# Attention and a gated MLP in one kernel: the causal mask moved to GpSimd after the exponential, the first head's bias rows taken from the sums, and a load issued earlier

## The chip, the core and the metric

The kernel runs on one core of a Trainium2 chip. The core has a matrix engine (TensorE, in the profile PE, with its weight loads as PEld), a vector engine (VectorE, DVE), an activation engine (ScalarE, ACT), a programmable engine (GpSimd, POOL) and a queue engine (SyncE, SP). They run side by side, each through its own list of instructions in order, and wait for each other on semaphores. DMA transfers are issued from SP, ACT or POOL. The metric is the time of one execution on the device in microseconds.

## The reference, cut to what matters

The first half is attention over 8 batches of 8 heads, 576 positions and 64 features a head. To each score comes a bias that is made from running sums of a gate s, and the scores above the diagonal are shut out:

```
s_pos = np.maximum(s, 0.0)
cum = np.cumsum(s_pos, axis=-1)
bias = -(cum[:, :, :, None] - cum[:, :, None, :])
scores = np.where(causal, -1000000000.0, scores + np.minimum(bias, 0.0))
attn = np.exp(scores - max); attn = attn / (sum + 1e-09)
x = attn @ v
```

The second half is an MLP over the 4608 tokens so made (8 heads of 64 are 512 features): `h = x @ w_in` (2048 wide), `g = h * clip(h + 3, 0, 6) / 6`, `out = g @ w_out`.

## The kernel before, in words

**Pairs of heads.** The 64 heads are worked on two at a time. The main loop runs over 32 pairs p, numbered from 0; the ninth is p = 8. For each head of a pair TensorE makes the transposed scores, with keys on the partitions. Only the blocks of 128 on and below the diagonal are made: the four full diagonal blocks in one PSUM bank (g = 0), the blocks below it in two more (g = 1, for key blocks 0 and 3, and g = 2, for 1 and 2), and the last 64 queries of both heads in one `corner`. ScalarE takes the exponential of each bank into the tile `P` (or `PC` for the corner), which has one buffer for each of three heads (two for the corner). Then `av` multiplies P by the values, which carry a column of ones for the sum, in 15 blocks of 65 columns: part 0 takes the four diagonal blocks and those below the diagonal of key block 0, part 1 the others and the corner. `norm` on VectorE divides by the sum into `x`.

**The bias.** The running sums enter the product itself, as extra rows 64 to 67 of the q and k tiles `qks` (four buffers). They come from `rows_of`, where the sum is held in several half-precision pieces (`cum1` to `cum6`: relu and scale on ScalarE, a scan on VectorE, the main piece by `cum3`, then the remainders), and reach `qks` by small DMAs, `load_aug`. The sums of the heads 0 to 31 are made at the start, those of the others during pairs 11 to 14. The first pair does not wait for these DMAs: its bias is added by separate products with `rows_of` and the tile `picked`, which holds the query side of one head, selected by a column of `sel`.

**The mask.** In the pairs 0 to 7 (`by_product`) a product of `ident2` and `shut` puts a large negative number above the diagonal before the scores are added. From p = 8 on, the rows 68 to 127 of q and k hold a staircase (`stair_sb`), so that the score product itself brings down most of what has to be shut out between 128-wide groups, and what is above the diagonal within a block is cut on VectorE after the exponential, by a minimum with a tile of 0 and 65504 (lines 358 and 390; the tile is made from `shut` in line 862).

**Getting q and k onto the partitions.** For p < 11 they are loaded and cast to half precision by a GpSimd DMA into `tok`, transposed on TensorE (L243) and copied out by VectorE and ScalarE (`transpose_out`, L260; `head_out`, L274 for the first pair). From p = 11 a DMA on SP transposes them (`crossbar_qk`, L287) into `jt`, and VectorE spreads that into `qks` (L220). From p = 18 the load is a plain DMA on SP into `raw`, and GpSimd casts (`cast_qk`, L192). The values are loaded by SP and cast by GpSimd (`cast_v`, L196 and L197).

**The MLP in between.** From p = 4 on, `group()` puts MLP work between the pieces of attention: `m1` (four products into `ph`, L473; relu of h + 3 on ScalarE, L488; the product with h on VectorE, `gT`, L489) and `m2` (L500, with `ob` on VectorE and the store on SP). `ph` has two buffers. The order is written out by hand in `plan` and then follows what is ready; it depends on counts alone, not on times. After the last pair only MLP work is left.

**The order.** The schedule is manual: each engine runs its instructions in the order in which the Python code emits them. In particular GpSimd's list per pair is, before the change, the loads or casts of q and k of later pairs, `cast_v(p + 1)`, and `load_aug(p + 2)`, all emitted at the head of the pair.

Of the kernel before, what the change touches and what calls it, by code (L numbers as in the profile page):

```python
# [11 lines left out]
AF = mybir.ActivationFunctionType  # L12
# [6 lines left out]
def kernel(  # L19
# [32 lines left out]
    NROW = 1  # L52
    NWARM = (11, 2, 5)
    HALVES = (slice(0, 288), slice(288, SEQ))
# [37 lines left out]
    shut = keep("shut", [128, 640], F16)  # L92
    masks = shut
    ident2 = keep("ident2", [128, 128], F16)
# [216 lines left out]
    def scores(p, hh, g):  # L311
# [44 lines left out]
        nc.scalar.activation(out=pt[:, c], in_=S, func=AF.Exp, scale=0.125)  # L356
        if g == 0 and not by_product:
            nc.vector.tensor_tensor(  # L358
                out=pt[:, c], in0=pt[:, c], in1=masks[:, c], op=ALU.min
            )  # L360

    def corner(p):
# [25 lines left out]
        )  # L388
        if not by_product:
            nc.vector.tensor_tensor(out=pc, in0=pc, in1=masks[:, 512:640], op=ALU.min)  # L390

# [4 lines left out]
    def av(p, hh, part):  # L396
        va, pt = vas[p % NVA], Pof(p, hh)
        if part == 0:

            tag = "o" if not hh or NPROD - 1 <= p < NPE - 2 else "po" if p < NPROD else "t"  # L400
            O[p, hh] = psum.tile(
                [128, 5, 65], F32, tag=tag, bufs=2 if tag == "po" else 1, name="O"
            )
        o = O[p, hh]

        def block(i, j, lhsT, **kw):
            mm(o[:, i, :], lhsT=lhsT, rhs=va[:, hh, j, 0:65], **kw)  # L407

        def off(i, j):
            c = OFF[j] + 128 * (i - j - 1)  # L410
            block(i, j, pt[:, c : c + 128], start=False, stop=False)
# [213 lines left out]

    fill(nc.vector, xT[:, 0, 0:512], 0.0)

# [86 lines left out]
    for c in HALVES:  # L714
        cum1(0, c)
    for c in HALVES:
# [24 lines left out]
    cast_v(0)  # L741
    for i in range(2):
        load_qk(2, i)
    for i in range(2):
# [7 lines left out]

    I, U = load_w_in, load_w_out
    for p in range(NP):
        nxt = p + 1 < NP
# [21 lines left out]
        elif p:  # L777
            qk_ahead()
            if NPE <= p + 2 < NP:
                if p + 2 >= NSW:  # L780
                    cast_qk(p + 2)
                crossbar_qk(p + 2)
            for fn, c in {
                4: ((I, 2),),
                5: ((I, 3),),
                6: ((U, 0), (U, 1), (U, 2), (U, 3)),
                7: ((U, 4), (U, 5), (U, 6), (U, 7)),
            }.get(p, ()):
                fn(c)
            if nxt:  # L790
                cast_v(p + 1)
            if p in (5, 6, 7):
                set_stair((p + 3) % NQK, nc.gpsimd.tensor_copy)
            if p == 4:
                load_aug(7, nc.gpsimd)
            elif p in (6, 7, 8) or 9 < p < NP - 2 and p != 14:
# [8 lines left out]
        whole = slice(0, SEQ)  # L805
        if p == 13:
            new_rest()
            cum4(1, nc.gpsimd, whole)
            cum5(1, nc.gpsimd.tensor_copy, whole)
        if p == 14:  # L810
            cum6(1, nc.gpsimd, whole)
            load_aug(16, nc.gpsimd)

# [46 lines left out]
        else:  # L860
            if p == NPROD:
                nc.vector.tensor_scalar(
                    out=masks, in0=shut, scalar1=65504.0, scalar2=None, op0=ALU.add
                )
            scores(p, 0, 0)
            get(0)
            group()
# [89 lines left out]
```

## Time and profile before

Three timed runs gave 357.73, 357.74 and 358.48 us, a median of 357.74. The profiled execution has a span of 356.7 us at a full TensorE clock.

| engine | busy us | share of the span |
|---|---|---|
| TensorE | 345.7 | 97% |
| VectorE | 250.7 | 70% |
| ScalarE | 224.4 | 63% |
| GpSimd | 133.9 | 38% |

The stretches of the kernel differ: up to about 10 us the sums are made and the first loads land; the pairs 0 to 3 run to 28 us; attention and MLP are mixed until about 273 us; the rest is MLP alone. Busy time by stretch, in us:

| stretch | TensorE | VectorE | ScalarE | GpSimd |
|---|---|---|---|---|
| 0 to 10 | 6.88 | 7.43 | 5.54 | 7.34 |
| 10 to 20 | 8.62 | 8.06 | 8.51 | 10.00 |
| 20 to 30 | 9.29 | 9.48 | 8.26 | 7.31 |
| 100 to 110 | 9.71 | 8.41 | 7.68 | 8.12 |
| 110 to 120 | 9.53 | 9.04 | 6.75 | 5.76 |
| 180 to 220 | 40.00 | 30.15 | 27.47 | 15.34 |

In a line of the profile, an entry such as `P<-S 128x512` names the tile written, the tile read and the shape; `x46` is a count; after the bar stand the busy time, the mean of one in ns, and the idle time ahead of it with what ended it. In a list of waits the three numbers are the total in us, how often, and the longest. In a timeline a row can hold several instructions of one kind; its first number is the start of the first, its second the time from that to the end of the last.

### The profile page before, as it was taken

How to read it: one execution, taken by the hardware profiler on the slowest of the kernel's cores; microseconds unless marked ns; L12 is line 12 of the kernel's file. 1: busy time of each engine (PE TensorE's matmuls, PEld its weight loads, DVE VectorE, ACT ScalarE, POOL GpSimd, SP SyncE). 2: the span in 40 equal slices, each digit the busy share in tenths (PEclk: the TensorE clock that was granted, in tenths of full speed). 3: DMA queues.
4: the chain of work that ended last, by engine and by line, in shares of the span. 5: the costliest groups of instructions: out<-in, count | busy, mean ns of one | idle time of the engine just before them, and what ended most of it. 6: DMA issues, size and time to landing. Idle time of an engine off the chain costs nothing.

```text
span 356.7 us, 7743 instructions
## 1 busy us (share of the span) xinstructions
PE 345.7 (97%) x2925; PEld 191.2 (54%) x2925; DVE 250.7 (70%) x544; ACT 224.4 (63%) x396; POOL 133.9 (38%) x223
## 2 busy tenths in 40 slices
PE   7799999999999999999999999999999999999995
PEld 2675666555555555555555555555555444444442
DVE  7798898877989876777777677878665544544531
ACT  5887987687786677666666666666664334443310
POOL 7977799675257342433333425252000000000000
PEclk9999999999999999999999999999999999999999
DMA  8799999999999998989789969897121101101111
GB/s 161 120 218 214 192 167 196 145 177 184 149 122 131 208 173 182 177 190 175 183 180 166 181 157 204 161 197 157 40 77 20 59 21 40 59 2 60 59 60 62
DMA packets 144439, 48.36 MB, mean 136 GB/s; under 512 B 130696, under 2 KB 139432, under 8 KB 144400
## 3 DMA queue, kind: packets, MB, share of 16 engines
q1 hardware_dynamic: 117088, 37.52, 51.9%
q0 software_dynamic: 27072, 10.05, 24.1%
q8 instruction: 23, 0.38, 0.5%
q10 hardware_dynamic: 240, 0.28, 0.2%
q14 instruction: 16, 0.13, 0.2%
HBM read 37.36 MB, written 9.44 MB: 131 GB/s over the span
## 4 chain that ended last, share of the span: by engine, by line
PE 86%; DVE 6%; ACT 2%; DMA 2%; issue 1%; POOL 1%; ACTq 0%; DVEq 0%
PE po L500 33%; PE ph L473 32%; PE O L407 7%; PE S L337 7%; PE S L322 3%; DVE gT L489 1%; DMA tok<-in_q_dram 1%; DVE qk L220 1%; PE pt L243 1%; PE ptx L444 1%; DVE qk L260 1%; DVE x L430 1%; ACT P L356 1%; DMA s_all<-in_s_dram 1%; PE S L319 1%
## 5 line engine op out<-in xcount | busy, mean ns | idle before, releaser
L489 DVE SCALAR_TENSOR_TENSOR gT<-tr,ph 128x512 f16<-128x512 f32 x144 | 98.9, 687 | 78.8 <-ACT tr L488 77.5
L473 PE MATMUL ph<-xT,w_in_sb 128*128 128x512 f16 x576 | 148.1, 379 | 0.9 <-DVE gT L489 0.8
L500 PE MATMUL po<-w_out_sb,gT 128*128 128x512 f16 x576 | 145.8, 379 | 0.0
L488 ACT ACTIVATE tr<-ph,bias 128x512 f32<-128x512 f32 x144 | 99.0, 687 | 74.3 <-PE ph L473 72.6
L356 ACT ACTIVATE P<-S 128x512 f16<-128x512 f32 x192 | 111.3, 595 | 38.1 <-PE S L337 19.1
L473 PEld LDWEIGHTS <-w_in_sb 128*128 128x128 f16 x576 | 51.7, 97 | 45.6 <-issue 1.2
L500 PEld LDWEIGHTS <-gT 128*128 128x128 f16 x576 | 50.2, 98 | 46.3 <-issue 0.2
L337 PE MATMUL S<-qk 68*128 68x448 f16 (+3 forms) x256 | 49.1, 272 | 0.3 <-ACT P L356 0.2
L407 PE MATMUL O<-va,P 128*128 128x65 f16 x896 | 47.8, 193 | 0.0
L407 PEld LDWEIGHTS <-P 128*128 128x128 f16 x896 | 39.3, 97 | 13.5
L196 POOL CAST va<-vraw 128x512 f16<-128x512 f32 x32 | 20.3, 633 | 52.7 <-DMA vraw<-in_v_dram 33.2
L152 POOL DMA_DIRECT2D qk<-rows_of x58 | 34.4, 595 | 9.3 <-ACT qk L619 5.2
L337 PEld LDWEIGHTS <-qk 68*128 68x128 f16 x256 | 23.7, 98 | 24.1 <-issue 0.7
L192 POOL CAST tok<-raw 128x576 f16<-128x576 f32 x28 | 19.4, 693 | 43.6 <-DMA raw<-in_q_dram 36.5
L220 DVE COPY qk<-jt 64x768 f16<-64x768 f16 x84 | 32.8, 391 | 1.2
L430 DVE TENSOR_TENSOR x<-O,rl 128x320 f16<-128x320 f32 x64 | 31.5, 492 | 2.2
L516 DVE TENSOR_SCALAR ob<-po 128x512 f32<-128x512 f32 (+1 forms) x36 | 24.4, 678 | 8.3 <-PE po L500 7.7
L322 PEld LDWEIGHTS <-qk 128*128 128x128 f16 (+1 forms) x256 | 18.9, 98 | 14.3 <-DVE qk L274 1.6
L260 DVE COPY qk<-pt 64x576 f16<-64x576 f16 x30 | 24.2, 805 | 3.0 <-PE pt L243 1.7
L322 PE MATMUL S<-qk 128*128 128x128 f16 (+1 forms) x256 | 24.8, 219 | 1.2 <-DVE qk L274 1.2
L358 DVE TENSOR_TENSOR P<-P,shut 128x512 f16<-128x512 f16 x48 | 21.0, 438 | 5.1 <-ACT P L356 4.9
L407 PE MATMUL O<-va,PC 128*128 128x65 f16 x64 | 12.3, 193 | 0.0
(70 smaller groups left out, 190.8 us busy)
## 6 DMA issues: line engine op xcount, KB each, us to landing
out_dram<-ob SPq DMA_DIRECT2D x35, 256.0 KB, 2.2
vraw<-in_v_dram SPq DMA_DIRECT2D x64, 128.0 KB, 3.6
raw<-in_q_dram SPq DMA_DIRECT2D x14, 288.0 KB, 3.6
raw<-in_k_dram SPq DMA_DIRECT2D x14, 288.0 KB
tok<-in_q_dram POOLq DMA_DIRECT2D x18, 144.0 KB, 5.3
tok<-in_k_dram POOLq DMA_DIRECT2D x18, 144.0 KB, 5.3
w_in_sb<-in_moe_w_in_dram POOLq DMA_DIRECT2D x4, 512.0 KB, 8.8
w_out_sb<-in_moe_w_out_dram POOLq DMA_DIRECT2D x8, 256.0 KB, 6.9
```

The costliest lines, as they stand in the source:

```text
L152: eng.dma_start(out=qks[p % NQK][64:68, hh, :, 64 * hh : 64 * hh + SEQ], in_=rows_of[g // 32].rearrange("(r g) i t -> g r i t", g=32)[g % ...
L220: copies[par](out=qk[0:64, :, i, 128 * par : 128 * par + 256 * n].rearrange("p h (s two c) -> p h s two c", two=2, c=128)[:, :, :, 0, :], ...
L260: copies[par](out=bass.AP(to.tensor, to.offset, [list(to.ap[0]), [2 * SPAD + 64, 2], [6, 96], [2, 3]],), in_=pt[64 * par : 64 * par + 64, ...
L322: mm(S[:, c], lhsT=kT[rows, c], rhs=qT[rows, c], start=(j == 0 and not by_product), stop=(j == 3 and p >= NROW),)
L337: mm(S[:, c : c + w], lhsT=kT[0:68, 128 * j : 128 * (j + 1)], rhs=qT[0:68, 128 * (j + 1) : SEQ], start=(c == 0), stop=(c != 0 and p >= NROW),)
L356: nc.scalar.activation(out=pt[:, c], in_=S, func=AF.Exp, scale=0.125)
L407: mm(o[:, i, :], lhsT=lhsT, rhs=va[:, hh, j, 0:65], **kw)
L430: nc.vector.tensor_tensor(out=X[p][:, :, hh, :], in0=o[:, :, 0:64], in1=rl.to_broadcast([128, 5, 64]), op=ALU.mult,)
L473: mm(ph, lhsT=w_in_sb[:, kc, ft * 128 : (ft + 1) * 128], rhs=xT[:, kc, n * 512 : (n + 1) * 512], start=(kc == 0), stop=(kc == NKC - 1),)
L488: nc.scalar.activation(out=tr, in_=ph, func=AF.Relu, bias=bias3[:, 0:1])
L489: nc.vector.scalar_tensor_tensor(out=gTs[n][:, ft, :], in0=tr, scalar=6.0, in1=ph, op0=ALU.min, op1=ALU.mult)
L500: mm(po, lhsT=gTs[n][:, ft, t4 * 128 : (t4 + 1) * 128], rhs=w_out_sb[:, ft, :], start=(ft == 0), stop=(ft == NFT - 1),)
```

## The change

**The mask.** VectorE's two minimums and the set-up of their tile are removed. A helper `shut_out` issues an `affine_select` on GpSimd that writes 0 into P above the diagonal, for the same 512 columns of each head and the 128 of the corner, for p >= 8. GpSimd's work of these pairs is put into two functions: `pool_mid`, emitted after the first head's g = 0 scores (the select of that head, `cast_v`, the first two steps of the second sums' remainders at p = 13), and `pool_end`, emitted after the second head's g = 0 scores (the select of the corner and of the second head, the last step of the remainders at p = 14, and `load_aug(p + 2)`). The loads and casts of q and k stay at the head of the pair.

**The order of AV.** Part 0 now takes the four blocks of key block 0 and the block (4, 3); part 1 takes the other five off the diagonal, then the four diagonal blocks and the corner. This holds for all pairs.

**The first head's picked rows.** They were made on VectorE from `rows_of`. Now ScalarE first fills the tile with the column of `sel` (an Identity of zeros with that bias), and then scales the sums of rows 0 to 31 into it in two halves. VectorE takes both k copies of the first head, and one copy more of the second head's q. The copy of the sums into `rows_of` on GpSimd is emitted later. There is one more warming product on TensorE, and the zeros that it uses are 576 wide.

**The third pair's loads** of q and k (`load_qk(2, i)`) are emitted on GpSimd ahead of that copy and ahead of the first `load_aug`.

```
-    NWARM = (11, 2, 5)
+    NWARM = (11, 2, 6)
...
-        if g == 0 and not by_product:
-            nc.vector.tensor_tensor(
-                out=pt[:, c], in0=pt[:, c], in1=masks[:, c], op=ALU.min
-            )
+
+    def shut_out(ap, w):
+        part = ap.rearrange("p (t c) -> p t c", c=w)
+        nc.gpsimd.affine_select(
+            out=part, in_=part, pattern=[[0, part.shape[1]], [1, w]],
+            compare_op=ALU.is_ge, fill=0.0, base=0, channel_multiplier=-1,
+        )
...
-        if not by_product:
-            nc.vector.tensor_tensor(out=pc, in0=pc, in1=masks[:, 512:640], op=ALU.min)
...
         if part == 0:
+            for i, j in ((1, 0), (2, 0), (3, 0), (4, 0), (4, 3)):
+                off(i, j, start=(i == 1))
+        else:
+            for i, j in ((2, 1), (3, 1), (4, 1), (3, 2), (4, 2)):
+                off(i, j)
             for j in range(4):
-                block(j, j, pt[:, 128 * j : 128 * (j + 1)], start=(j == 0), stop=False)
-            for i in range(1, 5):
-                off(i, 0)
-        else:
-            for i, j in ((2, 1), (3, 1), (4, 1), (3, 2), (4, 2), (4, 3)):
-                off(i, j)
+                block(j, j, pt[:, 128 * j : 128 * (j + 1)], start=False, stop=False)
...
-    fill(nc.vector, xT[:, 0, 0:512], 0.0)
+    fill(nc.vector, xT[:, 0, 0:SEQ], 0.0)
...
+    nc.scalar.activation(
+        out=picked[:, 0, :], in_=xT[:, 0, 0:SEQ], func=AF.Identity, bias=sel[:, 0:1]
+    )
...
+    def pick_first(cols):
+        nc.scalar.activation(
+            out=picked[0:32, 0, cols], in_=C["c"][0:32, cols],
+            func=AF.Identity, scale=sel[0:32, 0:1],
+        )
     for c in HALVES:
         cum2(c)
-        cum3(0, A, c)
-    nc.gpsimd.tensor_copy(out=rows_of[0][0:32, 0, 0:SEQ], in_=C["c"][0:32])
+    cum3(0, A, HALVES[0])
+    pick_first(HALVES[0])
+    cum3(0, A, HALVES[1])
     fill(nc.gpsimd, rows_of[0][0:32, 1, 0:SEQ], -1.0)
+    for i in range(2):
+        load_qk(2, i)
...
+    pick_first(HALVES[1])
+    nc.gpsimd.tensor_copy(out=rows_of[0][0:32, 0, 0:SEQ], in_=C["c"][0:32])
     pts = [transpose_in(0, 0)]
     head_out(0, 0, 0, pts[0], (A, A))
     warm(NWARM[1])
     pts.append(transpose_in(0, 1))
-    pick(0)
-    head_out(0, 1, 0, pts[1], (A, V.tensor_copy))
-    head_out(0, 0, 1, pts[0], (A, A))
+    head_out(0, 1, 0, pts[1], (V.tensor_copy, V.tensor_copy))
+    head_out(0, 0, 1, pts[0], (A, V.tensor_copy))
...
     cast_v(0)
     for i in range(2):
-        load_qk(2, i)
-    for i in range(2):
         load_qk(3, i)
...
+        def pool_mid():
+            if p >= NPROD:
+                shut_out(Pof(p, 0)[:, 0:512], 128)
+            if nxt:
+                cast_v(p + 1)
+            if p in (5, 6, 7):
+                set_stair((p + 3) % NQK, nc.gpsimd.tensor_copy)
+            if p == 13:
+                new_rest()
+                cum4(1, nc.gpsimd, whole)
+                cum5(1, nc.gpsimd.tensor_copy, whole)
+
+        def pool_end():
+            if p >= NPROD:
+                shut_out(PCs[p % 2][:, 0:128], 64)
+                shut_out(Pof(p, 1)[:, 0:512], 128)
+            if p >= NPROD and p != 9 and p + 2 < NP:
+                if p == 14:
+                    cum6(1, nc.gpsimd, whole)
+                load_aug(p + 2, nc.gpsimd)
...
-            if p == NPROD:
-                nc.vector.tensor_scalar(
-                    out=masks, in0=shut, scalar1=65504.0, scalar2=None, op0=ALU.add
-                )
             scores(p, 0, 0)
+            if p >= NPROD:
+                pool_mid()
             get(0)
...
         scores(p, 1, 0)
+        if p >= NPROD:
+            pool_end()
```

More of the change, by code (lines that the diff above doesn't have):

```diff
@@ L92 @@
     shut = keep("shut", [128, 640], F16)
-    masks = shut
     ident2 = keep("ident2", [128, 128], F16)
@@ L356, in scores @@
         nc.scalar.activation(out=pt[:, c], in_=S, func=AF.Exp, scale=0.125)
-        if g == 0 and not by_product:
-            nc.vector.tensor_tensor(
-                out=pt[:, c], in0=pt[:, c], in1=masks[:, c], op=ALU.min
-            )
+    def shut_out(ap, w):
+        part = ap.rearrange("p (t c) -> p t c", c=w)
+        nc.gpsimd.affine_select(
+            out=part,
+            in_=part,
+            pattern=[[0, part.shape[1]], [1, w]],
+            compare_op=ALU.is_ge,
+            fill=0.0,
+            base=0,
+            channel_multiplier=-1,
+        )
     def corner(p):
@@ L407, in block, with off @@
             mm(o[:, i, :], lhsT=lhsT, rhs=va[:, hh, j, 0:65], **kw)
-        def off(i, j):
+        def off(i, j, start=False):
             c = OFF[j] + 128 * (i - j - 1)
-            block(i, j, pt[:, c : c + 128], start=False, stop=False)
+            block(i, j, pt[:, c : c + 128], start=start, stop=False)
         if part == 0:
-            for j in range(4):
-                block(j, j, pt[:, 128 * j : 128 * (j + 1)], start=(j == 0), stop=False)
-            for i in range(1, 5):
-                off(i, 0)
-        else:
-            for i, j in ((2, 1), (3, 1), (4, 1), (3, 2), (4, 2), (4, 3)):
-                off(i, j)
+            for i, j in ((1, 0), (2, 0), (3, 0), (4, 0), (4, 3)):
[3 more added lines that the diff above has]
+                off(i, j)
+            for j in range(4):
+                block(j, j, pt[:, 128 * j : 128 * (j + 1)], start=False, stop=False)
             c = 64 * hh
@@ L715 @@
         cum1(0, c)
+    def pick_first(cols):
+        nc.scalar.activation(
+            out=picked[0:32, 0, cols],
+            in_=C["c"][0:32, cols],
+            func=AF.Identity,
+            scale=sel[0:32, 0:1],
+        )
     for c in HALVES:
         cum2(c)
-        cum3(0, A, c)
-    nc.gpsimd.tensor_copy(out=rows_of[0][0:32, 0, 0:SEQ], in_=C["c"][0:32])
+    cum3(0, A, HALVES[0])
+    pick_first(HALVES[0])
+    cum3(0, A, HALVES[1])
     fill(nc.gpsimd, rows_of[0][0:32, 1, 0:SEQ], -1.0)
+    for i in range(2):
+        load_qk(2, i)
     new_rest()
@@ L753 @@
     I, U = load_w_in, load_w_out
+    whole = slice(0, SEQ)
     for p in range(NP):
@@ L782 @@
                 crossbar_qk(p + 2)
+        def pool_mid():
[17 more added lines that the diff above has]
+                load_aug(p + 2, nc.gpsimd)
+        if p >= PPB:
             for fn, c in {
@@ L789 @@
                 fn(c)
[L790 to L793, printed above, removed]
+        if PPB <= p < NPROD:
+            pool_mid()
             if p == 4:
                 load_aug(7, nc.gpsimd)
-            elif p in (6, 7, 8) or 9 < p < NP - 2 and p != 14:
+            elif p in (6, 7):
                 load_aug(p + 2, nc.gpsimd)
@@ L804 @@
             fill(nc.gpsimd, rows_of[1][:, 0, :], 1.0)
[L805 to L812, printed above, removed]
         if p == NPROD + 1:
@@ L860 @@
         else:
-            if p == NPROD:
-                nc.vector.tensor_scalar(
-                    out=masks, in0=shut, scalar1=65504.0, scalar2=None, op0=ALU.add
-                )
             scores(p, 0, 0)
+            if p >= NPROD:
+                pool_mid()
             get(0)
```

## The prediction

> **What bounds the kernel now.** I read the page first, then what TensorE waited for, then the timelines of the stretches where it waited.
>
> ```profile
> PE 345.7 (97%) x2925; PEld 191.2 (54%) x2925; DVE 250.7 (70%) x544; ACT 224.4 (63%) x396; POOL 133.9 (38%) x223
> PE 86%; DVE 6%; ACT 2%; DMA 2%; issue 1%; POOL 1%; ACTq 0%; DVEq 0%
> ```
>
> TensorE (PE) is the path: 86% of the chain that ended last. The other engines count only where PE stands still. The waits of PE name the places:
>
> ```profile
> PE S L322 <- DVE qk L274: 1.2, 1, 1.2
> PE ptx L444 <- DVE x L430: 1.0, 3, 0.4
> PE pt L243 <- DMA tok<-in_k_dram: 0.9, 1, 0.9
> PE pt L243 <- DMA tok<-in_q_dram: 0.9, 1, 0.9
> PE ph L473 <- DVE gT L489: 0.8, 2, 0.5
> ```
>
> A busy matmul row overlaps its neighbours, so I also compared starts: from the start of one group of matmuls to the next, against the same group undisturbed (four 128-column scores take 0.22 us in the chain, two 448/64-column ones 0.22). Lost in this way: about 1.0 us before the third pair's transposes, 1.3 us before the first score, and after 70 us the following.
>
> ```profile
> 104.34 0.39 PE L322 MATMUL S<-qk 128*128 128x128 f16 x4
> 105.02 1.02 PE L473 MATMUL ph<-xT,w_in_sb 128*128 128x512 f16 x4 [0.29 <-DVE gT L489]
> ...
> 113.15 0.39 PE L322 MATMUL S<-qk 128*128 128x128 f16 x4
> 114.01 1.02 PE L473 MATMUL ph<-xT,w_in_sb 128*128 128x512 f16 x4 [0.47 <-DVE gT L489]
> ```
>
> 105.02 - 104.34 - 0.22 = 0.46 us; 114.01 - 113.15 - 0.22 = 0.64; likewise 0.16 at 116.6 and 0.19 at 76.2. All four wait for VectorE's gT: 1.45 us. One more, 0.27 us at 73.1, waits for ScalarE. From 120 to 341 us PE loses about 0.1 us in 10; nothing is to be had there. VectorE ahead of the largest stall:
>
> ```profile
> 111.06 0.53 DVE L358 TENSOR_TENSOR P<-P,shut 128x512 f16<-128x512 f16 x1
> 111.50 1.74 DVE L220 COPY qk<-jt 64x768 f16<-64x768 f16 x2
> 113.27 0.69 DVE L489 SCALAR_TENSOR_TENSOR gT<-tr,ph 128x512 f16<-128x512 f32 x1
> ```
>
> The mask's min stands ahead of two copies and the gT that PE wants. At the start, VectorE, then GpSimd:
>
> ```profile
> 14.70 0.49 DVE L430 TENSOR_TENSOR x<-O,rl 128x320 f16<-128x320 f32 x1
> 16.42 1.64 DVE L260 COPY qk<-pt 64x576 f16<-64x576 f16 x2 [1.23 <-PE pt L243]
> ```
>
> ```profile
> 9.29 1.18 POOL L152 DMA_DIRECT2D qk<-rows_of  x2 [1.63 <-DVE w_out_sb L704]
> 11.36 0.66 POOL L117 DMA_DIRECT2D tok<-in_q_dram  x1
> 12.01 0.67 POOL L117 DMA_DIRECT2D tok<-in_k_dram  x1
> ```
>
> The third pair's q and k are issued at 11.36 and 12.01; PE's transposes of q start at 15.96, when it lands, and VectorE idles 1.23 us behind them. From 9.5 to 12 us the DMA engines moved 15 GB/s in the mean, against 136 over the span.
>
> **What the Trainium skill says.** GPSIMD Engine Reference, Engine selection: one-input elementwise work runs at about line rate on GpSimd. The trace agrees: a select of 128x512 f16 (L607) took 630 ns, of 128x128 288 ns; VectorE's min took 438. SBUF — State Buffer, Who interferes with whom: a VectorE instruction with two SBUF inputs, or a copy in a two-port mode, and a GpSimd instruction that reads SBUF exclude each other for a whole instruction. The trace agrees: the chain has the first subtraction L682 at 0.46 us and the second, beside a GpSimd cast, at 0.93. ScalarE: Activation LUTs, Table sets: identity is in every set, so the new Identity calls should load no table; no run shows it yet.
>
> **The change part by part.** Pairs are numbered from 0, as in the code: the third is pair 2.
>
> Start. *Picked rows.* Gone: VectorE's 0.37 us pick between the bias rows and the head's copies. Added on ScalarE: one 128x576 Identity (0.65 us, by the 128x576 cast of L679) once sel is there at 3.0; ScalarE waits for s until 4.1, so it costs nothing; and two 32x288 scalings (0.43 each, by L679's halves). The first runs at 5.81, in ScalarE's gap to 6.30. The second stands ahead of the head's copies: +0.43 on ScalarE. *Cast of the sums* (L719, POOL, 6.73 to 7.38): moved behind the loads, so the second L682 should take 0.46 in place of 0.93, as only a memset (0.33) runs beside it: -0.47. So the residual rows end near 8.2 (8.65 before), the second scaling near 8.1, ScalarE's two q copies (0.46 each) near 9.0, VectorE's two k copies (0.50 each, now without a copy on ScalarE ahead) near 9.25. First score 9.25 instead of 10.22. But VectorE now makes five of the eight head copies, before three: 8.2 + 5 x 0.50 + 0.25 waiting for ScalarE = 10.95, then the second pick (0.48) to 11.45, against 11.57 before. The 0.25 us wait before 13.49 also goes. The second pair's scores thus gain only about 0.35 of the 0.97. *Loads.* Two GpSimd issues of 0.65 move to 7.06 - 8.4, behind the memset; the cast (0.65) and the bias-row loads follow at 9.05, against 9.29, and cast_v(0) at 10.2, against 10.46: nothing behind them is late. SP's bias rows for the third pair now wait for that cast, until 9.05 rather than 8.65; they are used after 18 us. A load took 3.6 to 9.1 us, median 5.9; from 8.4 even 5.9 is 14.3, before the transposes want it (14.7). The fourth pair's load then issues 1.3 us earlier. VectorE's copies start after the transposes near 15.1, against 16.42: the start gains 1.3 us in all. That is a chain on VectorE (9.48 of 10 us busy from 20 to 30), so it is carried on; w_in's first block lands at 25.0 and is wanted at 29.1, so it is not what comes next. One more warm matmul (0.22) ends before 9.1, and the wider memset costs 0.03 before work that waits for s: nothing. Bounds: 0.35, if a load is late, to 1.7.
>
> *Mask.* VectorE loses 48 x 0.438 + 24 x 0.318 + 0.32 (mask set-up) = 29.0 us; GpSimd gets 48 x 0.63 + 24 x 0.288 = 37.2. Per pair: VectorE -1.2, GpSimd +1.55. Of the first only the stalls count. The 0.46 at 105 should go: without the min the copies start 0.4 to 0.7 earlier. Of the 0.64 at 114 I take 0.4, as the copies (1.74 for two, where 0.66 is usual) are held by GpSimd, and the load issues of pair 17 plus a select still stand there. With 0.16 and 0.15 of 0.19 this makes 1.2 us. Bounds: 0.3 (the copies run into selects) and 1.8 (ScalarE's stall goes too).
>
> *What waits for the select.* AV's diagonal blocks move to its second half, 15 blocks in all as before: same PE time. In pair 24 the first exp ends at 199.1, the select could be done by 199.8, and the diagonal blocks run at about 206.2: 6.4 us of slack; for the second head 203.7, 204.7 with the corner, and 210: 5 us. The tightest is pair 13: the select queues behind two load issues to 104.7, wanted at 108.3. *What waits behind it on GpSimd:* cast_v (wanted in the next pair), load_aug (now near 206 instead of 200.6; wanted at 216.5), the issues of q and k for pairs 11 to 17 (up to 7 us later in pair 12, wanted two pairs on), and from pair 16 the casts of q and k, which feed SP's transposing DMA. The remainder of the second sums moves too: its first two steps (1.28 and 0.88 us) behind pair 13's select, its last (1.34) behind pair 14's second select, to about 116.9, so that the bias rows of pair 16 are issued to 118.1 and, with 3.7 us to land, are there near 122, wanted at 126.9. In pairs 24 and 25 the casts of q and k ended at 196.6 and 204.8, and will end near 198.1 and 207.3; the transposes issue at 200.3 and 211.7. All hidden by PE.
>
> Sum against the profiled span of 356.7: 1.3 + 1.2 = 2.5, so 354.2. The timed runs lie at 357.73 to 358.48; I take 2.5 from the median, 357.74: 355.2.
>
> **The rivals.**
> 1. *Only the start gains.* The copies of L220 collide with selects, or ScalarE's two long casts at 100 us set the 105 us stall. For: copies beside GpSimd take 0.83 and 0.95, not 0.36. Against: the min had two SBUF inputs and collided as well (corner mins of 0.68 and 0.76 us). 357.74 - 1.3 = 356.4.
> 2. *Only the mask gains.* The early load lands late, or the five VectorE copies eat it. Against: empty DMA engines at 10 us. 357.74 - 1.2 = 356.5.
> 3. *Slower: GpSimd and SP hold each other.* From pair 16 a cast waits for the select of the pair before, SP's transposing DMA for the cast, and the next raw load queues behind that DMA on SP; the next cast, with a select behind it, waits for the load. It decides once casts slip by more than the 3.7 us between cast (196.6) and transpose (200.3); I estimate 1.5 to 2.5. Speaking for it:
>
> ```profile
> POOL tok L192 <- DMA raw<-in_q_dram: 36.5, 14, 5.6
> ```
>
>    A slip of 0.3 us beyond the slack in each of 14 pairs is 4.2: 355.2 + 4.2 = 359.4.
> 4. *No change:* neither stall moves, as other waits take their places: 357.7.
>
> **How the numbers follow.** Both parts 0.62; only the start 0.15; only the mask 0.08; slower 0.09; no change 0.06. About 0.2% (0.7 us) is what a measurement of this kernel can tell from no change. Rivals 1 and 2 still lie beyond it, so faster is 0.62 + 0.15 + 0.08 = 0.85, same 0.06, slower 0.09. The range goes from 354.0 (both parts near their upper bounds, 3.5 less their improbable ends) to 356.9, which takes in rivals 1 and 2; out of it lie rivals 3 and 4. The likeliest case alone: 354.2 to 356.0.
>
> **What would show it.** Right: first score near 9.3 us; no wait of PE for tok after 14 us; VectorE busy near 222 us, GpSimd near 171; PE's wait for gT under 0.4; no waits of PE for POOL. Wrong: a line "PE O <- POOL P", casts of q and k ending after their transposes' old places, a second table load on ScalarE, or stalls at 105 and 114 of unchanged size.

## The result, and the profile after

The changed kernel took 356.24 us (median of four runs, 356.18 to 356.27), the kernel before 358.11 (median of four, 357.73 to 358.91): a ratio of 0.9945, 95% interval 0.9925 to 0.9964. The forecast was 355.2, range 354.0 to 356.9. The profiled spans are 354.5 and 356.7: 2.2 us less, where the sum said 2.5. The runs of the kernel before scatter over 1.2 us, those of the changed one over 0.1.

Its page, busy time of the engines and the chain by engine:

```profile
PE 345.6 (97%) x2926; PEld 191.5 (54%) x2926; DVE 231.5 (65%) x472; ACT 225.4 (64%) x397; POOL 169.6 (48%) x295
PE 90%; DVE 4%; ACT 3%; issue 1%; DMA 1%; ACTq 0%
```

TensorE's share of the chain rose from 86% to 90%, VectorE's fell from 6% to 4%, and GpSimd, which had 1%, is gone from it. What TensorE waited for in the changed kernel (total in us, times, longest):

```profile
PE ptx L449 <- DVE x L435: 1.3, 3, 0.5
PE Sc L302 <- DVE w_out_sb L712: 0.7, 1, 0.7
PE pt L242 <- DMA tok<-in_k_dram: 0.5, 1, 0.5
PE O L412 <- ACT P L355: 0.3, 1, 0.3
```

The waits for the head's qk (1.2), for gT (0.8) and for the third pair's tok (0.9) are gone; the tok wait that is left is at 7.4 us, for the first pair. A line is new: the wait for the second head's picked rows, L712. None names GpSimd. The timeline of TensorE at the start (start, length, then the operation; in brackets the idle time and its releaser):

```profile
9.36 0.40 PE L321 MATMUL S<-qk 68*128 68x128 f16 x4
...
11.08 0.20 PE L385 MATMUL Sc<-qk 68*128 68x64 f16 x1
11.93 0.19 PE L302 MATMUL Sc<-w_out_sb,rows_of 128*128 128x64 f16 x1 [0.65 <-DVE w_out_sb L712]
...
12.47 0.39 PE L321 MATMUL S<-qk 68*128 68x128 f16 x4
```

The first score starts at 9.36 (10.22 before), but the second head's scores at 12.47, as they did before. The same two places that stalled behind gT, at 104 to 105 and 113 to 114 us before:

```profile
103.28 0.39 PE L321 MATMUL S<-qk 128*128 128x128 f16 x4
103.51 1.03 PE L478 MATMUL ph<-xT,w_in_sb 128*128 128x512 f16 x4
...
111.69 0.39 PE L321 MATMUL S<-qk 128*128 128x128 f16 x4
111.92 1.03 PE L478 MATMUL ph<-xT,w_in_sb 128*128 128x512 f16 x4
```

From scores to the next product it is 0.23 us at both, the undisturbed 0.22. Where the 2.2 us arose is read from the same matmul in both traces, the first diagonal score of a head. "Lead" is how much earlier the changed kernel reaches it:

| place | lead, us |
|---|---|
| pair 0, first head | 0.86 |
| pair 0, second head; pair 1, first head | 0.01 |
| pair 1, second head | 1.05 |
| pair 5 | 0.93 |
| pair 8; pair 12 | 1.21; 1.22 |
| pair 13 | 1.06 |
| pair 14 | 1.46 |
| pair 15; pair 31 | 2.11; 2.15 |

Three pieces: 1.05 at the start (the third pair's tok is there), 0.29 in pairs 5 to 7, 1.05 between pairs 13 and 15 (the two stalls), less 0.12 lost by pair 5 and 0.16 at pair 12. So the two pictures fit the two parts of the forecast. The experiments show that the pictures mislead in both.

### The profile page after: what moved, and what is told of

It is laid out like the page before. It is cut to its first block, busy times and chain, and to the rows that moved or that the text cites. A ratio compares the mean times of both kernels' runs of the same rounds, so it can differ in the third digit from the quotient of the medians.

```text
span 354.5 us, 7771 instructions
## 1 busy us (share of the span) xinstructions
PE 345.6 (97%) x2926; PEld 191.5 (54%) x2926; DVE 231.5 (65%) x472; ACT 225.4 (64%) x397; POOL 169.6 (48%) x295
## 4 chain that ended last, share of the span: by engine, by line
PE 90%; DVE 4%; ACT 3%; issue 1%; DMA 1%; ACTq 0%
PE po L505 34%; PE ph L478 34%; PE O L412 8%; PE S L336 7%; PE S L321 4%; DVE qk L259 1%; PE pt L242 1%; ACT P L355 1%; PE ptx L449 1%; DMA s_all<-in_s_dram 1%; DVE x L435 1%; PE S L318 1%; ACT tr L493 1%; DVE qk L219 1%; PE Sc L385 0%
## 5 line engine op out<-in xcount | busy, mean ns | idle before, releaser
L355 ACT ACTIVATE P<-S 128x512 f16<-128x512 f32 x192 | 111.4, 596 | 37.4 <-PE S L321 22.2
L359 POOL TENSOR_SCALAR_AFFINE_SELECT P<-P 128x512 f16<-128x512 f16 x48 | 31.2, 650 | 45.2 <-ACT P L355 45.1
L219 DVE COPY qk<-jt 64x768 f16<-64x768 f16 x84 | 36.6, 437 | 1.2
L359 POOL TENSOR_SCALAR_AFFINE_SELECT PC<-PC 128x128 f16<-128x128 f16 x24 | 7.1, 294 | 41.0 <-ACT PC L393 40.9
L195 POOL CAST va<-vraw 128x512 f16<-128x512 f32 x32 | 21.2, 664 | 3.4 <-DMA vraw<-in_v_dram 3.3
L191 POOL CAST tok<-raw 128x576 f16<-128x576 f32 x28 | 18.1, 681 | 0.0
```

Of the source, the lines that this page charges most:

```text
L219: copies[par](out=qk[0:64, :, i, 128 * par : 128 * par + 256 * n].rearrange("p h (s two c) -> p h s two c", two=2, c=128)[:, :, :, 0, :], ...
L359: nc.gpsimd.affine_select(out=part, in_=part, pattern=[[0, part.shape[1]], [1, w]], compare_op=ALU.is_ge, fill=0.0, base=0, channel_multip ...
```

## The experiments

The kernels ran in three groups, each on one chip with its own runs of the kernel before. Their medians differ by chip, so ratios are compared between groups and times within one.

| kernel | us, median (range, runs) | ratio to before, 95% |
|---|---|---|
| before, first group | 357.25 (356.25 to 359.38, 37) | |
| changed | 356.10 (356.03 to 356.30, 9) | 0.9964 (0.9950 to 0.9978) |
| mask alone | 356.94 (356.27 to 357.83, 22) | 0.9989 (0.9980 to 0.9998) |
| start alone | 356.25 (356.18 to 357.20, 13) | 0.9971 (0.9960 to 0.9982) |
| changed, second pick ahead | 355.51 (355.44 to 355.76, 6) | 0.9945 (0.9927 to 0.9964) |
| before, second group | 357.81 (356.36 to 359.37, 39) | |
| before, GpSimd's steps moved | 357.29 (356.58 to 358.61, 22) | 0.9987 (0.9977 to 0.9998) |
| before, without the minimums | 356.63 (355.92 to 357.79, 12) | 0.9972 (0.9957 to 0.9987) |
| changed, load late | 356.30 (356.06 to 357.59, 12) | 0.9963 (0.9947 to 0.9980) |
| before, third group | 357.23 (356.23 to 359.29, 29) | |
| before, early load alone | 356.89 (355.92 to 358.31, 22) | 0.9987 (0.9975 to 0.9999) |
| changed, every select four times | 390.21 (389.41 to 390.55, 4) | 1.0922 (1.0898 to 1.0947) |
| second pick ahead, AV order of before | 355.68 (355.54 to 357.06, 8) | 0.9962 (0.9945 to 0.9979) |
| second pick ahead, staircase on VectorE | 355.26 (355.15 to 355.39, 6) | 0.9947 (0.9931 to 0.9964) |

### The changed kernel again, for comparison

> The changed kernel once more, unaltered, as the partner for the other kernels of this call. Span expected at 354.5 us, as in its first profile, and a time 0.4 to 0.6% under the kernel before.

356.10 and a span of 354.4. On this chip the kernel before gains 1.15 us in the median.

### The mask alone

The start of the kernel before, with the new mask and AV order.

```
-    cum3(0, A, HALVES[0])
-    pick_first(HALVES[0])
-    cum3(0, A, HALVES[1])
+        cum3(0, A, c)
...
+    pick(0)
...
+    for i in range(2):
+        load_qk(2, i)
```

> The start of the kernel before, with the new mask and the new order of AV. Theory (two gains that add: about 1.0 us from the start, up to the first score of pair 4, and about 1.1 us from the mask, between 98 and 118 us): span 355.4 to 355.8, the stalls of TensorE at about 105 and 114 us gone. Rival A (only the start gains, the rest is the run's own scatter): 356.7, stalls unchanged. Rival B (the mask gives everything): 354.5.

Measured: 356.94, which is 0.31 us below the kernel before. Both stalls are gone from its trace (0.14 us left at 114.8), and against the first profile of the kernel before it leads by 0.59 us at pair 8 and 1.52 at pair 15. The trace says 0.9 us between them, the runs 0.3 in all: the profile it was compared with was not typical of the kernel before. The execution in that first profile took 358.45 us at a full clock. Of the 105 runs of the kernel before in the three groups six took as long, and these six had a mean clock of 0.993 to 0.995.

### The start alone

The new start, with the mask on VectorE and the old AV order.

```
-            if p >= NPROD:
-                shut_out(Pof(p, 0)[:, 0:512], 128)
...
+        if g == 0 and not by_product:
+            nc.vector.tensor_tensor(
+                out=pt[:, c], in0=pt[:, c], in1=masks[:, c], op=ALU.min
+            )
```

> The new start, with the mask on VectorE and the order of AV of the kernel before. Theory (1.0 us from the start, carried to the end): span 355.5 to 355.9, pair 4's first score near 27.2 us, stalls at about 104 and 112 us still there with 0.4 and 0.6 us. Rival (the stalls after 100 us hang on the start: an earlier start moves them apart from the second sums and they go too): 354.5. Rival (start gain given back at the stalls): 356.7.

Measured: 356.25, span 354.4: 1.00 us below the kernel before, and only 0.15 above the changed one. With every minimum in place the two stalls are gone here too. So the minimums alone did not make them. VectorE in this kernel at the second place:

```profile
109.38 0.41 DVE L358 TENSOR_TENSOR P<-P,shut 128x512 f16<-128x512 f16 x1
109.72 1.07 DVE L220 COPY qk<-jt 64x768 f16<-64x768 f16 x2
110.81 0.69 DVE L489 SCALAR_TENSOR_TENSOR gT<-tr,ph 128x512 f16<-128x512 f32 x1
```

and in the changed kernel:

```profile
109.45 1.45 DVE L219 COPY qk<-jt 64x768 f16<-64x768 f16 x2
110.93 0.69 DVE L494 SCALAR_TENSOR_TENSOR gT<-tr,ph 128x512 f16<-128x512 f32 x1
```

The minimum (0.34 us up to the next start) is gone, and the two copies took 0.38 longer: gT starts at 110.93 and 110.81, no earlier. GpSimd beside them, in the changed kernel:

```profile
109.76 1.03 POOL L128 DMA_DIRECT2D tok<-in_k_dram  x1
110.77 0.68 POOL L359 TENSOR_SCALAR_AFFINE_SELECT P<-P 128x512 f16<-128x512 f16 x1
```

The second copy ran from 109.96 to 110.90 and ended 0.12 us after the load's issue did. In the start-alone kernel both issues were over at 109.52, and the copies met only casts. In the changed one the issues come 1.25 us later (108.72 against 107.47), because the previous pair's select and bias rows now stand ahead of them. The mask's time came off VectorE and put GpSimd's issues where VectorE's copies run.

### The kernel before, a second profile

No edit.

> The kernel before once more, for a second profile. Theory (the 1.1 us lost at 104 and 113 us is a collision: VectorE's copies of L220 and GpSimd's work hold each other, and who comes first is a matter of chance): the two stalls have other sizes than 0.46 and 0.64 us, with the copies' durations moving with them (0.66 us for a pair of copies when free, up to 1.9 when held), and the wait for the third pair's load another size than 1.0. Rival (the stalls are the min's own and fixed): the same two sizes to 0.1 us.

Measured: 356.89 us, span 355.1. Its two stalls at 104 and 113 us are absent and its wait for the third pair's tok, counted from start to start, is 0.53 us instead of 1.03. VectorE at the same place:

```profile
110.38 1.07 DVE L220 COPY qk<-jt 64x768 f16<-64x768 f16 x2
```

1.07 us, where the first profile has 1.74. What GpSimd did beside that 1.74, in the first profile of the kernel before:

```profile
111.39 1.34 POOL L694 TENSOR_TENSOR rows_of<-r,rows_of 32x576 f16<-32x576 f32 x1
```

The first of the two copies started at 111.50, 0.11 us behind this subtraction, and ended at 112.94, 0.22 behind its end. In the start-alone kernel the subtraction started at 110.71 and the copies were over at 110.78. Some tenths of a microsecond decide whether a copy of 0.3 us takes 1.4. This agrees with the Trainium skill, SBUF — State Buffer, Who interferes with whom, which says that the order of issue and not the shape of the operation decides who is blocked. At the first place it was the issues of two loads (from 102.08 and 103.12) that held two copies, of 0.91 and 0.96 us; in the second profile only one of the two was held (0.74). The two profiles of the kernel before differ by 1.6 us, which is the two stalls (0.46 + 0.64) and the landing of one load (0.5). The trace of the kernel with the early load alone, further down, has neither stall either (0.22 us from the scores to the next product at both places). So of the four traces with the old mask and GpSimd's old order in these pairs only the first has them.

### The kernel before with GpSimd's steps moved

The last step of the second sums goes from pair 14 to 15, pair 16's loads of q and k from pair 13 to 12; the minimums stay.

```
+                if p == 15:
+                    cum6(1, nc.gpsimd, slice(0, SEQ))
+                    load_aug(16, nc.gpsimd)
...
-        if p == 14:
-            cum6(1, nc.gpsimd, whole)
-            load_aug(16, nc.gpsimd)
+        if p == 12:
+            for i in range(2):
+                load_qk(16, i)
```

> The kernel before with two pieces of GpSimd's work moved in time and nothing else: pair 16's loads are issued in pair 12 instead of 13, and the last step of the second sums with pair 16's bias rows in pair 15 instead of 14. Mask and start as before. Theory (collision): the copies at 111.5 us are free (0.7 us for two) and the stall at 113 us of 0.64 goes; at 104 us a cast and bias-row loads still stand beside the copies, so that 0.46 shrinks or stays; 0.5 to 1.0 us less than the kernel before, of the same size as the mask's part. Rival (VectorE has too much work there and only the min's removal helps): stalls unchanged, no gain.

Measured: 357.29 against 357.81. Copies of VectorE in this kernel:

```profile
104.02 1.76 DVE L220 COPY qk<-jt 64x768 f16<-64x768 f16 x2
...
111.00 0.65 DVE L220 COPY qk<-jt 64x768 f16<-64x768 f16 x2
```

At 111 us nothing runs on GpSimd, two copies take 0.65 us behind an unchanged minimum, and the stall there is gone. At 104 us another subtraction stands beside them, and they take 1.76:

```profile
104.36 1.27 POOL L682 TENSOR_TENSOR r<-c,rows_of 64x576 f32<-64x576 f32 x1
```

That GpSimd's row and not the minimum makes a copy long is thus shown from both sides. The stall at 104 is gone too, as these long copies stand behind gT there and not ahead of it. In exchange a stall of 0.6 us at 96 us and one of 0.24 at 107 appeared, so the gain stays at half a microsecond.

### The kernel before without the minimums

Both minimums are left out, so the part above the diagonal of pairs 8 to 31 is not shut out.

```
-        if g == 0 and not by_product:
-            nc.vector.tensor_tensor(
-                out=pt[:, c], in0=pt[:, c], in1=masks[:, c], op=ALU.min
-            )
...
-        if not by_product:
-            nc.vector.tensor_tensor(out=pc, in0=pc, in1=masks[:, 512:640], op=ALU.min)
```

> The kernel before with both minimums of the mask left out (the part above the diagonal is then not shut out), nothing added on GpSimd. It bounds what any cheaper mask could give. Theory: TensorE is the path, so only stalls at 76, 104, 113 and 116 us go: at most 1.45 us under the kernel before, in the mean of many runs 0.3 to 0.8. Rival (VectorE's 29 us matter all along): more than 2 us.

Measured: 0.9972 (0.9957 to 0.9987), so 0.5 to 1.5 us is what the minimums cost the kernel before if nothing takes their place (1.2 between the medians, above the 0.3 to 0.8 expected). The mask alone gave 0.9989 (0.9980 to 0.9998). The intervals just overlap; that GpSimd takes back part of the gain fits them but is not settled by them.

### The third pair's load late

The changed kernel, with that load put back behind the bias rows.

```
-    for i in range(2):
-        load_qk(2, i)
     new_rest()
...
     cast_v(0)
+    for i in range(2):
+        load_qk(2, i)
```

> The changed kernel with the third pair's loads put back behind the bias rows and the values' cast; picked rows, copies and mask as changed. Theory (the start's gain is the load alone, since the first score's 0.86 us is lost at the second head): TensorE waits for tok at about 15 us again, pair 1's second head starts near 17.5 instead of 16.45, the time falls back to that of the kernel with the new mask alone, 356.9, with its wide scatter. Rival (the earlier first score holds some of it): 356.3 to 356.6.

Measured: 0.9963, the changed kernel's own ratio. q was issued at 11.07 us and landed at 14.58, k at 16.31, and TensorE shows the wait:

```profile
16.36 0.43 PE L242 MATMUL pt<-ident,tok 96*128 96x96 f16 x6 [0.50 <-DMA tok<-in_k_dram]
```

It costs nothing by the end. The theory that the start's gain is the early issue falls: with the rest of the new start in place, the load may be issued late. Two things stay open. No run separates the early picked rows from the rest of it (the other sharing of the copies, the later cast of the sums). And in this trace q landed at 14.58, where the five traces with the old start and the load at its old place have 15.3 to 15.9; its issue was only 0.3 to 0.6 us earlier, and why it landed so early isn't shown.

### The early load alone

The kernel before, with the load at its new place.

```
     fill(nc.gpsimd, rows_of[0][0:32, 1, 0:SEQ], -1.0)
+    for i in range(2):
+        load_qk(2, i)
     new_rest()
```

> The kernel before with the third pair's loads issued ahead of the bias rows and nothing else: picked rows, copies, mask and order of AV as before. With the loads late but the picks changed, the start had kept nearly all of its gain, so this asks the other half. Theory A (the landing of these loads sets the start, and the picked rows only make room for it): TensorE does not wait for tok after 14 us, pair 2's first score near 18.7 instead of 19.7, span 355.4 to 355.8 with the stalls near 104 and 113 us as chance has it. Theory B (the two overlap: without the changed picks, VectorE's copies for the second and third pairs are now the later of the two): pair 2's first score at 19.1 to 19.4. Rival (the bias rows of pair 1 come 1.3 us later and hold its scores): pair 1 later than 14.5 us, no gain.

Measured: 356.89 against 357.23, but in two heaps: ten runs at 355.92 to 356.65, twelve at 356.87 to 358.31. The profiled run, 357.98, is of the second. Its busy time by stretch (TensorE, weight loads, VectorE, ScalarE, GpSimd; then TensorE's granted clock, DMA share, GB/s), and the row of TensorE ahead of it:

```profile
12.00:13.00 1.00, 1.00 (x13) 0.88 (x12) 0.99 (x2) 0.79 (x3) 1.00 (x3) 0.50 0.69 159
13.00:14.00 1.00, 1.00 (x9) 0.84 (x8) 0.42 (x2) 0.77 (x1) 1.00 (x3) 0.50 0.73 100
```

```profile
10.24 0.40 PE L322 MATMUL S<-qk 68*128 68x128 f16 x4 [1.76 <-DVE qk L274]
```

TensorE stood for 1.76 us before the first score, and its clock then fell to half from about 11.7 to 15.1 us. The second pair's scores came at 16.11, where the kernel before had 14.48. The load itself had landed early (q at 11.1 us). In the traces with the new start TensorE stands for 0.7 us at most there, and in the changed kernel its clock is 1.00 in every stretch from 8 to 16 us. Of the twelve long runs three have a mean clock of 0.995 over the span (357.95 to 358.31, this one among them); why the other nine are long isn't shown.

### The second head's pick ahead of its copies

The changed kernel, with the pick ahead of the second head's three VectorE copies.

```
     head_out(0, 1, 0, pts[1], (V.tensor_copy, V.tensor_copy))
+    pick(1)
     head_out(0, 0, 1, pts[0], (A, V.tensor_copy))
...
-    for g in range(1, 2 * NROW):
-        pick(g)
```

> The changed kernel with the second head's pick on VectorE ahead of that head's three copies, where VectorE now idles 0.46 us for ScalarE. Theory (in the changed kernel TensorE stands 0.8 us at the corner for that pick, so the 0.86 us by which the first score is earlier is lost again at the second head): the wait of TensorE for the picked rows goes, the second head's first score moves from 12.47 to about 11.8 us, pair 4's from 27.2 to 26.6 to 26.9, span 353.9 to 354.3. Rival (VectorE's copies for pair 1 are what counts and they start no earlier, or the copy of the sums on GpSimd at 9.1 us holds the pick back): span 354.5.

Measured: 355.51, 0.59 below the changed kernel on the same chip. VectorE:

```profile
9.31 0.37 DVE L712 TENSOR_SCALAR w_out_sb<-rows_of,sel 128x576 f16<-128x576 f16 x1
```

The wait for L712 is gone, the second head's scores start at 11.83 (12.47), and a lead of 0.62 us is still there at pair 4. So most of the 0.86 us gained before the first score was lost at that one wait.

### Every select four times

```
-        nc.gpsimd.affine_select(
+        for _ in range(4):
+            nc.gpsimd.affine_select(
```

> The changed kernel with every select done four times over, which changes no value: 3 x 1.55 = 4.65 us more of GpSimd in each pair from 8 on, so that it comes to about 8.9 of the pair's 9.2 us in the pairs from 18 on, and over the pair's time in the pairs 8 to 17. Theory (the select has 3 to 6 us of slack and the transposes 3.7): the pairs from 18 on lose little, those from 8 to 17, where the slack was 3 to 5 us, lose some 0.5 to 1.5 us each, 5 to 12 us in all, and TensorE waits for the select by name. Rival (the select is hidden wherever it stands): under 1 us.

Measured: 390.21 us, with a span 33.7 us above the changed kernel's. TensorE's waits:

```profile
PE O L413 <- POOL PC L360: 22.4, 21, 3.1
```

The wait is for the corner's select. The turning point exists, but I sized it badly. From 140 to 180 us the changed kernel's GpSimd is busy 22.2 of 40 us, so 5.1 of a pair's 9.2, and 4.1 us are free (20.0 of 40 from 180 to 220). Three more rounds add 3 x (2 x 0.65 + 0.29) = 4.8: 9.9 us, over the edge. From pair 19 on each pair loses about 0.8 us, after 21.7 lost by the first score of pair 17, where GpSimd has more to do. I had left out that it adds up from pair to pair. Not all of it is the select: from 109.7, 123.4 and 143.9 us TensorE's clock was 0.50 for 3.4 us each. TensorE was busy in these stretches, so half of their 10.2 us, 5.1 of the 33.7 at most, is my estimate of the clock's share.

### The old order of AV

The kernel with the second pick ahead, and AV as before.

```
-            for i, j in ((1, 0), (2, 0), (3, 0), (4, 0), (4, 3)):
-                off(i, j, start=(i == 1))
+            for j in range(4):
+                block(j, j, pt[:, 128 * j : 128 * (j + 1)], start=(j == 0), stop=False)
+            for i in range(1, 5):
+                off(i, 0)
```

> The kernel with the second pick ahead, with AV in the order of the kernel before: diagonal blocks in the first half, which then waits for the select. Theory (the select has 0.9 to 4 us of slack even there, and three blocks fewer stand between the last product and the division): TensorE's wait of 0.27 us at 95 us falls to 0.12, those at 30.6 and near 39 us come back in their old sizes (0.37 and 0.24), no waits for the select but 0.1 to 0.3 in pair 8; span 353.8 to 354.2, a draw. Rival (the order matters: the select is late for the first half): waits for the select in pairs 8 to 15, 1 to 4 us more.

Measured: 0.9962 (0.9945 to 0.9979), against 0.9945 (0.9927 to 0.9964) on another chip for the new order: no difference that these intervals tell. The waits of about 0.15 to 0.24 us behind gT at 38, 45 and 53 us came back, so the 0.29 us in pairs 5 to 7 were the AV order's. In exchange TensorE's waits for x come to 1.0 us with the old order and to 1.3 with the new one: it gives and takes. The wait of 0.27 us at 95 us stayed, against what was expected, so the 0.16 us lost at pair 12 isn't the AV order's.

### The staircase on VectorE

The kernel with the second pick ahead; in pairs 8 and 9 VectorE, not ScalarE, writes the staircase.

```
-            set_stair(3, nc.scalar.copy, (p - 8,))
+            set_stair(3, nc.vector.tensor_copy, (p - 8,))
```

> The kernel with the second pick ahead, and the staircase of the last q and k buffer written by VectorE in pairs 8 and 9 instead of ScalarE, as VectorE is only 64% busy from 60 to 70 us since it has no mask. Theory (0.76 us on ScalarE hold back an exponential there and with it the scores): TensorE's stall of 0.37 us at 71 us goes, span 353.5 to 353.7. Rival (the copy on VectorE collides with GpSimd and holds gT instead): stall of the same size behind gT, 353.9 or more.

Measured: 355.26, span 353.4, ratio 0.9947: the shortest span of all, and 0.42 us below the kernel with the old AV order on the same chip. The stall behind ScalarE at 71 us is gone; one of 0.30 us behind gT appears at 77. Its span is 1.1 us below the changed kernel's. The kernel with the old AV order differs in two things, though, and the kernel with the second pick ahead and the new order had 0.9945 on its chip. So the runs do not show that the staircase's move gains time.

## Why the prediction was right, step by step

**The forecast as a whole.** The measured time lies in the range, and the two spans agree with the sum (2.2 against 2.5). In part that is luck. Over many runs the gain is 1.15 us (ratio 0.9964), less than half of 2.5, and the sum priced stalls of a profile that was not typical of its kernel. The lower end of the range doesn't follow from its reason either: 354.0 lies 3.7 below 357.74, while the two upper bounds add up to 3.5.

**First score at 9.25.** 9.36: right, and nearly by the steps given (the two scalings took 0.53 us each, not 0.43). The changed kernel loads one table on ScalarE, at 1.74 us, as the kernel before does, so the new Identity calls loaded none.

**"The second pair's scores gain only about 0.35 of the 0.97".** This step failed. They gained 0.01, and so did the second head. I compared the second pick's end, 11.45, with 11.57 before, and never asked who waits for it. VectorE finished it later still:

```profile
11.31 0.57 DVE L712 TENSOR_SCALAR w_out_sb<-rows_of,sel 128x576 f16<-128x576 f16 x1
```

The corner's second bias product wants it. Before, TensorE came there at 11.94, when the pick was done; now it comes at 11.1, and as it takes its work in order, all of the second head's scores stand behind this product until 11.93. The experiment with the pick ahead returns 0.6 of the 0.86.

**The load, and 1.3 us at the start.** Landing before 14.3: it landed at 11.0 and 12.0. VectorE's copies start at 15.38 instead of 16.42: 1.04, not 1.3. Alone, the start gave 1.00. But I had made the load the cause of what is left. The rest of the new start suffices (load late: 0.9963), with the reservation above on its landing; the early load suffices only in some runs (0.9987). So the two seem to cover the same time and don't add up. In the five traces with the old start and the load at its old place, q's landing varies (15.3 to 15.9 us), and its price with it.

**The mask, 1.2 us.** This term was mis-sized: in the runs it is 0.31 us alone and 0.15 on top of the start. The two stalls that I credited to it were there in the first profile, and gone in the changed one (1.05 us of the lead), so the sum came out. But that they were there was chance: they are gone also in the second profile of the kernel before, and in the start-alone kernel with all its minimums. They were collisions of VectorE's copies with GpSimd's rows. Of the 1.74 us the prediction says that "the copies are held by GpSimd", and still credits the mask with 0.4; its bound from below, 0.3 ("the copies run into selects"), is about what was measured. Left out with nothing in their place, the minimums were worth 0.5 to 1.5 us; how much of that GpSimd's rows take back, and how much the runs' chance makes of it, isn't settled.

**Busy times.** GpSimd 169.6 against 171: right. VectorE 231.5 against 222: wrong, since I multiplied counts by durations although such rows overlap by some 0.07 us (109.38 + 0.41 against a next start at 109.72), and the copies L219 rose from 32.8 to 36.6 us in all, and VectorE has two more of the first pair's head copies for one pick less, about 0.6 us.

**What waits for the select.** Right but for one place. The two selects took

```profile
L359 POOL TENSOR_SCALAR_AFFINE_SELECT P<-P 128x512 f16<-128x512 f16 x48 | 31.2, 650 | 45.2 <-ACT P L355 45.1
L359 POOL TENSOR_SCALAR_AFFINE_SELECT PC<-PC 128x128 f16<-128x128 f16 x24 | 7.1, 294 | 41.0 <-ACT PC L393 40.9
```

and in pair 24 were done 6.4 and 5.5 us before their blocks (6.4 and 5 forecast), in pair 13 3.2 and 3.1 us. Of these the tightest is pair 8 with 3.0 us, not 13. The forecast asked after the corner's select for the second head alone. For the first head it has nothing to spare in pair 13, as it stands behind the first two steps of the second sums on GpSimd:

```profile
106.67 0.30 POOL L359 TENSOR_SCALAR_AFFINE_SELECT PC<-PC 128x128 f16<-128x128 f16 x1
106.69 0.44 PE L412 MATMUL O<-va,P 128*128 128x65 f16 x9
107.02 0.20 PE L412 MATMUL O<-va,PC 128*128 128x65 f16 x1
```

The corner's product starts 0.06 us behind the select's end and 0.08 behind the product ahead of it, where 0.03 is usual: TensorE waited some 0.04 us, too little for a line among the waits. In the other pairs this select is done 2.1 to 3.6 us ahead. Casts of q and k in pairs 24 and 25 ended at 195.5 and 204.8, not later than before (196.6, 204.8), where 198.1 and 207.3 were forecast.

**The rivals.** "Only the start gains" (1.3 us) is nearest to what holds over many runs: start alone gains 1.00, the changed kernel 1.15. "Only the mask gains" (1.2) fell: 0.31. "GpSimd and SP hold each other" isn't near: no wait for GpSimd but the 0.04 us above, and 4 us of a pair free. "No change" fell.

**What stays open.** The wait of 0.27 us at 95 us, and which chance (landing, collision, clock) made each long run of the kernel before. That the changed kernel scatters so little fits a removal of all three; it isn't shown for each. For the clock there is this: of the 183 runs of kernels with the old start in the three groups, 12 had a mean clock of 0.993 to 0.995 and took 357.8 us or more; of the 54 with the new start, the fourfold select left out, none was under 0.997. Ahead of the first score TensorE stands for 1.2 to 1.8 us in the traces of the former and for 0.7 at most in those of the latter.

## What to carry to other kernels

A stall in one profile is worth what it is in many runs: before crediting an edit with it, take a second profile of the same kernel, and look at which rows of the other engine stand beside the long ones. When a step is sped up, follow the engine that consumes it in its own order to the next thing it waits for; the gain is lost at the first one that did not move. Two edits that each remove the same gap can be worth little more than one: here the start alone gave 1.00 us and the mask alone 0.31, both together 1.15.

## What the runs showed of the hardware

After TensorE had stood for 1.76 us near the start of the kernel with the early load alone, its clock was 0.50 for about 3.4 us (11.7 to 15.1). The kernel with every select done four times has three more such stretches of 3.4 us. Ahead of them TensorE had stood for 0.87 and 1.82 us, for 3.07, and for 1.82. But two stands of 1.8 us in that trace (at 85 and 96 us) and one of 1.68 in the kernel with GpSimd's steps moved (at 8.6) were followed by no fall, so the length of one stand does not decide it alone. The Trainium skill, TensorE: Matmul & The Clock Gate, Part 1, has the clock fall after an idle window of about 3.4 us, counted by a free-running window. The length of the four stretches at half clock agrees; the stands ahead of them, 1.8 to 3.1 us, were all shorter than the page's window, and the measurement decides.

A VectorE copy of 64x768 f16 takes 0.28 to 0.36 us when GpSimd is idle. One that is held ends 0.1 to 0.2 us behind the GpSimd row that it met: 0.94 us beside the issue of a DMA (1.03), 1.43 beside a subtraction (1.34). Not every copy that overlaps is held: in the start-alone kernel one that started at 101.15 took 0.35 within an issue from 100.87 to 102.06. That the issue of a load alone can hold a copy was not among my costs.
